# Values of the segments in DRAM: from one row for each token to blocks by group and half, stored whole

## The chip, the cores and the metric

The kernel runs on one core of a Trainium2 chip. The metric is the device time of one execution in microseconds (us). Three runs took 1616.81, 1618.66 and 1619.32 us; the median, 1618.66 us, is the time before. The profile is that of one further execution of 1616.37 us, 1614.70 of them the span from the first to the last instruction.

The engines are named as the profile does: PE (matrix products; PEld is its weight load), DVE (vector), ACT (activations and copies), POOL (general), SP (here nothing but a queue that issues DMAs in order). A name with a q behind it (SPq) is the engine's sequencer.

## What is computed

Four layers one after the other on x of 2048 tokens by 512, in bf16: attention with a recurrent memory (A), a dense layer (B), A again, B again, each on the layer-normed x and added to it. A goes through the tokens in 64 segments of 32:

```
mem = mem0                                   # 8 rows
for s in range(64):
    h = concat(mem, x[32*s : 32*s+32])       # 40 rows of 512
    q, k, v = h @ Wq, h @ Wk, h @ Wv         # 32 heads of 128: 4096 columns each
    p = softmax(mask(q @ k.T * scale))       # for each head 40 x 40
    o = (p @ v) @ Wo                         # back to 512
    mem = o[:8];  outs.append(o[8:])
```

B is `maximum(x @ w1, 0) @ w2` with 1376 columns in between. The memory makes the segments of one layer a chain.

## The kernel before, in words

**Steps.** The program is a chain of 68 steps, k = 0 to 67. In step k the first attention layer works on segment k, and from k = 4 on the second one on segment k - 4 (`layers`, L281), so that two chains share a step. The dense layer of step k is that of segment pair k - 2. A step has the products for queries and keys of half the heads (`qk`, L555: `qp` by L541, its copies QT on ACT L547 and KT on DVE L549), scores `sp` (L575), softmax (L586: `mx`, `es`, `sm`, `P_sb`), the other half likewise, the transposed probabilities (`tp` L617, or a transposing DMA L624), `pv` (L643, weights times the values `Vs`), the product with Wo (`wo` L583 for the memory rows, `wox` L374/L397/L402 for the others), the new memory `mt` and its copies, and last `memory_values(k + 1)` (L715), the values of the memory rows for the next step: two groups `vm` (L724), each copied by ACT into a tile VmS (L728) and stored in DRAM by SP (L729, which issues through `put`, L302).

**Who sets the order.** The instructions of PE, DVE, SP and POOL stand in the order in which the code writes them (`manual_schedule`, L959). Only ACT's order is chosen by the scheduler. Each engine, SP with its DMAs too, takes its instructions strictly one after the other.

**Where the values come from.** `Vs` has for each of the two layers 40 rows of 4096 values. The memory's 8 rows come from `vmd` (L734). The tokens' 32 rows come from DRAM too: for the second layer from `vd1` (`values1`, L342, loaded by L698); for the first layer in steps with k % 4 of 0 or 1 from `vmd` (L703), and in those with k % 4 of 2 or 3 from `vd0[k // 2]` (L706). There the values of a pair of segments (64 tokens) lie, computed ahead by `values0` (L304): one group is 1024 of the 4096 columns, in two halves of 512, one half in partitions 0 to 63 and the other in 64 to 127 of one PSUM tile. ACT copies it to a tile of 128 x 512 (L320), and SP stores each half (64 x 512, 64 KB) into its columns of a DRAM tensor of 64 rows by 4096.

**The first steps.** Step 0 has groups of `values0` for pairs 1, 3 and 5 beside its own work; their copies go to room in the still empty tiles of the dense weights, `w1_sb` and `w2_sb` (`slots`, L809), and their stores are held back (`put` with `later`, L298). In step 1 SP flushes the held stores (L876), 22 of values and 2 of memory values, and then issues the loads of the dense weights (`load_dense`, L156: w1 by L157, w2 by L158 and L160), which overwrite that room and so wait for the stores. Step 1 also has three groups of `values0` of its own (pair 5 group 6, pair 7 groups 0 and 2), whose tiles carry the tag vst, five buffers that VmS, the memory rows `wm` and some inputs use as well. Their 6 stores stand behind the weight loads in SP's queue. Then follow the two VmS stores of `memory_values(2)` at the end of step 1, and in step 2 the load L706, the transposition L289 (`xnT`, the normed tokens that the dense layer's `hp`, L477, reads), the loads L734 and the transposition L624.

**Later steps.** From step 5 on every fourth step (k % 4 = 1) has two to four groups of `values0` (`values_at`, L759).

Of the kernel before, what the change touches and what calls it, by code (L numbers as in the profile page):

```python
# [7 lines left out]
BF = mybir.dt.bfloat16  # L8
# [14 lines left out]
def kernel(  # L23
# [14 lines left out]
    nc = tc.nc  # L38
    _, S, Dm = A_x.shape
    _, H, Dh = A_Wq.shape[0], A_Wq.shape[1], A_Wq.shape[2]  # L40
    M = A_mem0.shape[1]
    SEG = int(A_seg_len)
    Dff = B_w1.shape[1]
    assert Dm == 512 and Dh == 128 and M == 8 and SEG == 32 and H == 32
    L = M + SEG
# [9 lines left out]
    NCH = H * Dh // 512  # L55
# [3 lines left out]
    dram = ctx.enter_context(tc.tile_pool(name="vdram", bufs=2, space=DRAM))  # L59
# [135 lines left out]
    Vs = const.tile([128, H * Dh], BF)  # L195
# [13 lines left out]
    for a in range(2):  # L209
        t = ps_s.tile([128, 512], F32, name=f"sp{a}")  # L210
# [4 lines left out]
    xT0, xnT_tiles, hT_tiles, vd0, vd1, vmds, wm_tiles, wo_tiles, xp_tiles, vp_tiles, obs = {}, {}, {}, {}, {}, {}, {}, {}, {}, {}, {}  # L215
# [82 lines left out]
    def put(later, **store):  # L298
        if later:
            held.append(store)  # L300
        else:
            nc.sync.dma_start(**store)  # L302

    def values0(p, n, lo=0, hi=NC4, pool=None, stage=None):  # L304
        r = 64 * (p % 2)
        if (n, lo) == (0, 0):
            vd0[p] = dram.tile([64, H * Dh], BF, tag="vd0", bufs=3, name="vd0")
        if lo == 0:
            pool, tag = (pool, "wo") if pool else (ps_fill, "fill")
            vp_tiles[p, n] = pool.tile([128, 512], F32, tag=tag, name="vp")  # L310
        vp = vp_tiles[p, n]
        for c4 in range(lo, hi):
            for j in range(2):
                nc.tensor.matmul(vp[64 * j:64 * j + 64, :], lhsT=xT0[p // 2][:, c4, r:r + 64],  # L314
                                 rhs=Wv_sb[:, c4, (n + j) * 512:(n + j + 1) * 512],
                                 start=(c4 == 0), stop=(c4 == NC4 - 1), tile_position=(0, 64 * j))
        if hi < NC4:
            return
        vst = wk.tile([128, 512], BF, tag="vst", bufs=5, name="vst")[:] if stage is None else stage
        nc.scalar.copy(out=vst, in_=vp[:])  # L320
        for j in range(2):
            put(stage is not None, out=vd0[p][:, (n + j) * 512:(n + j + 1) * 512], in_=vst[64 * j:64 * j + 64, :])

    def values_first(ii):

# [369 lines left out]
    def load_values(k, act):  # L695
        for a in act:
            if a == 1 or k == 1:
                nc.sync.dma_start(out=Vs[64 * a + M:64 * a + L, :].rearrange("t (n e) -> t n e", n=NCH),  # L698
                            in_=(vd1.pop(k) if a else vd0[0])[:].rearrange("i j t e -> t (i j) e"))
            elif k >= 4 and k % 4 < 2:  # L700
                for u in range(2):
                    lo = M + 2 * M * u
                    nc.sync.dma_start(out=Vs[lo:lo + 2 * M, :].rearrange("t (n e) -> t n e", n=NCH),  # L703
                                in_=vmds[k - k % 4 - 4 + 2 * (k % 4) + u][:, :, 2 * M:32, :].rearrange("i j t e -> t (i j) e"))
            else:
                nc.sync.dma_start(out=Vs[M:L, :], in_=vd0[k // 2][SEG * (k % 2):SEG * (k % 2) + SEG, :])  # L706

    def tokens_in(k):
        for a in range(2):
# [29 lines left out]
    def block(k, lo, hi):  # L739
        output_x(k - 1, lo, hi)  # L740
        groups = values_at(k)
        if split(k):

            rest = [(i, 0, NC4) for i in range(1, len(groups))]
            if k == 1:
                todo = [] if lo == 0 else [(0, 0, 2)] if hi == 16 else [(0, 2, NC4)] + rest
            else:
                todo = [(0, 0, 2)] if lo == 0 else [(0, 2, NC4)] if hi == 16 else rest
        else:
            todo = [(i, c4, c4 + 2) for i in range(len(groups)) for c4 in range(0, NC4, 2)  # L750
                    if lo < 8 * i + 2 * c4 + 2 <= hi]
        for i, c_lo, c_hi in todo:
            p, n = groups[i]
            values0(p, n, c_lo, c_hi, ps_wo if i in (0, 3 if len(groups) == 4 else 2) else None)
# [51 lines left out]
    def first_step():  # L806
# [5 lines left out]
        with tc.high_priority(offset=PRIO):  # L812
# [4 lines left out]
            memory_values(0, (next(slots), None), (0,))  # L817
            values_second(0, next(slots))
            values0(1, 0, stage=next(slots))
            values0(1, 2, stage=next(slots))  # L820
            m = moments_x(2)
            normalize(nc.vector, xbs[2], xbs[2], m, 0, 128)
# [25 lines left out]
    def step(k):  # L848
# [9 lines left out]
        with tc.high_priority(offset=PRIO):  # L858
            behind = norm_rows.pop(k, None)
            if k == 1:  # L860
                def behind():
                    normalize(nc.vector, xbs[n_x], xbs[n_x], moments_x(n_x), 0, 128)
            qks = qk(0, act, behind=behind)
            load_values(k, act)
            if k == 1:
                memory_values(k)
                inputs_T(n_x, True)
# [91 lines left out]
    with tc.manual_schedule(engines={mybir.EngineType.PE, mybir.EngineType.DVE, mybir.EngineType.SP,  # L959
# [30 lines left out]
        t = xnT_tiles[d + 2] = wk.tile([128, NC4, 128], BF, tag="xnT", bufs=1, name="xnT")  # L990
# [48 lines left out]
```

## Time and profile before

| what | value |
|---|---|
| median of 3 runs | 1618.66 us (1616.81 to 1619.32) |
| profiled execution | 1616.37 us, its span 1614.70 us |
| PE busy | 1568.4 us, 97% of the span |
| DVE, ACT, POOL busy | 1262.5, 738.0, 346.7 us (78%, 46%, 21%) |
| DMA, all queues | 146.41 MB, 91 GB/s in the mean |
| 64 KB stores of values (L302, vd) | 106 from vst tiles and 22 from the weights' room |
| loads L706 (256 KB each) | 32 |

How to read it. The page gives each engine's busy time, its busy share in 40 equal slices of the span (40.4 us each), and the chain of work that ended last, followed back from the last instruction. The waits list who waited for whom: total us, number of times, longest. The timeline has start, duration, engine, line, operation, output<-input and a count of merged instructions; a DMA's row there is the time that SP took to issue it, not the transfer. The chain of waits in order of time has start, duration, and engine or DMA with the line. The table by windows gives the busy time of each engine in a stretch, then three figures: the clock granted to PE (1.00 is full), the busy share of the 16 DMA engines, and GB/s. In the listing of one tile the three figures are minimum, median and maximum in ns of one instruction. The names `vd`, `VmS`, `w_sb` are the tiles with their numbers left out (`w_sb` is w1 or w2).

### The profile page before, as it was taken

Reading aid. Unit: us, or ns where it says so; the run is one execution under the profiler, and the core shown is the slowest. Engines: PE = TensorE matmul, PEld = TensorE weight load, DVE = VectorE, ACT = ScalarE, POOL = GpSimd, SP = SyncE. Lnnn points to the kernel's source line nnn. Section 1 sums busy time; section 2 is a strip of 40 time slices with the busy share of each in tenths; the row PEclk is TensorE's granted clock in tenths of the full one; section 3 lists DMA queues with packets and bytes.
Section 4 is the critical chain, followed back from the end, with each engine's and each line's share of the span. In section 5 each row is a group of like instructions: output and inputs, shape, how many; then the busy total and the mean of one; then the engine's idle time right before and its main releaser. Section 6 shows DMA issues by size and latency. Waiting matters only on the chain.

```text
span 1614.7 us, 94984 instructions
## 1 busy us (share of the span) xinstructions
PE 1568.4 (97%) x42782; PEld 1323.0 (82%) x42782; DVE 1262.5 (78%) x3112; ACT 738.0 (46%) x1800; POOL 346.7 (21%) x666
## 2 busy tenths in 40 slices
PE   6969999999999999999999999999999999999997
PEld 3657888888888888888889888888988888888876
DVE  4548888888888888888888888888888788887865
ACT  3424444454444444444444544445454544545443
POOL 2001122222222222222222222222222222222110
PEclk9979999999999999999999999999999999999999
DMA  9444334443443444343334334443443443334331
GB/s 367 140 132 81 88 63 96 85 83 70 92 86 70 86 90 88 61 94 83 82 75 93 88 65 94 89 83 71 90 92 78 78 87 78 77 76 96 72 67 40
DMA packets 216390, 146.41 MB, mean 91 GB/s; under 512 B 125000, under 2 KB 209328, under 8 KB 214960
## 3 DMA queue, kind: packets, MB, share of 16 engines
q1 hardware_dynamic: 212832, 136.10, 38.4%
q8 instruction: 336, 5.51, 1.5%
q0 software_dynamic: 3072, 4.20, 1.1%
q14 instruction: 70, 0.57, 0.2%
q10 hardware_dynamic: 80, 0.03, 0.0%
HBM read 65.41 MB, written 45.35 MB: 69 GB/s over the span
## 4 chain that ended last, share of the span: by engine, by line
PE 94%; DMA 2%; DVE 1%; SPq 1%; ACT 1%; issue 1%; POOLq 0%; ACTq 0%; DVEq 0%
PE qp L541 37%; PE wox L374 10%; PE wo L583 8%; PE vm L724 7%; PE v L355 7%; PE hp L477 6%; PE sp L500 5%; PE pv L643 4%; PE sp L575 4%; PE vp L314 3%; DMA Wv_sb<-in_A_Wv_dram 2%; PE tp L617 1%; PE xp L448 1%; PE wox L397 1%; DMA vd<-vst 0%
## 5 line engine op out<-in xcount | busy, mean ns | idle before, releaser
L547 ACT CAST QT<-qp 128x480 bf16<-128x480 f32 (+3 forms) x408 | 201.1, 493 | 394.3 <-PE qp L541 394.2
L541 PE MATMUL qp<-HT,Wq_sb 128*128 128x80 bf16 (+1 forms) x8704 | 369.8, 200 | 1.6 <-POOL HT L713 1.2
L541 PE MATMUL qp<-HT,Wk_sb 128*128 128x80 bf16 (+1 forms) x8704 | 369.0, 199 | 2.4 <-DVE KT L549 1.1
L541 PEld LDWEIGHTS <-Wq_sb 128*128 128x128 bf16 x8704 | 326.2, 99 | 33.3 <-issue 25.8
L541 PEld LDWEIGHTS <-Wk_sb 128*128 128x128 bf16 x8704 | 328.7, 100 | 3.6 <-issue 2.7
L549 DVE CAST KT<-qp 128x480 bf16<-128x480 f32 (+3 forms) x408 | 225.1, 565 | 102.1 <-PE qp L541 100.0
L607 POOL TENSOR_TENSOR P_sb<-es,sm 128x320 bf16<-128x320 f32 x185 | 130.5, 719 | 752.5 <-ACT es L597 501.4
L374 PE MATMUL wox<-Wo_sb,OTx 128*64 128x256 bf16 x2880 | 173.6, 273 | 0.0
L591 DVE TENSOR_REDUCE mx<-sp 128x8 f32<-128x320 f32 x256 | 114.7, 487 | 72.4 <-PE sp L575 71.6
L602 DVE TENSOR_REDUCE sm<-es 128x8 f32<-128x320 f32 x256 | 118.9, 465 | 44.3 <-ACT es L597 33.9
L374 PEld LDWEIGHTS <-OTx 128*64 128x64 bf16 x2880 | 150.1, 110 | 2.9
L597 ACT ACTIVATE es<-es 128x320 f32<-128x320 f32 x256 | 110.4, 468 | 60.2 <-DVE es L595 59.5
L724 PE MATMUL vm<-Wv_sb,HTm 128*32 128x512 bf16 x2176 | 136.4, 380 | 0.6 <-DVE HT L793 0.6
L355 PE MATMUL v<-Wv_sb,xnT 128*32 128x512 bf16 x2048 | 129.0, 378 | 0.5 <-PE wo L583 0.5
L583 PE MATMUL wo<-Wo_sb,OTm 128*32 128x512 bf16 x2144 | 128.9, 380 | 0.4 <-issue 0.4
L567 DVE CAST sp<-maskb 128x320 f32<-128x320 bf16 x256 | 118.4, 484 | 0.0
L477 PE MATMUL hp<-xnT,w_sb 128*128 128x64 bf16 (+3 forms) x2948 | 102.7, 193 | 14.4 <-DMA xnT<-XN 14.0
L595 DVE TENSOR_TENSOR es<-sp,mx 128x320 f32<-128x320 f32 x256 | 113.8, 483 | 1.6
L724 PEld LDWEIGHTS <-HTm 128*32 128x32 bf16 x2176 | 90.5, 96 | 27.4 <-issue 12.1
L477 PEld LDWEIGHTS <-w_sb 128*128 128x128 bf16 (+1 forms) x2948 | 95.5, 101 | 15.4 <-issue 9.8
L500 PE MATMUL sp<-w_sb,hT 128*64 128x256 bf16 (+4 forms) x1474 | 106.2, 277 | 0.5 <-ACT hT L483 0.5
L728 ACT CAST VmS<-vm 128x512 bf16<-128x512 f32 x134 | 78.4, 585 | 61.4 <-PE vm L724 54.0
(113 smaller groups left out, 2024.4 us busy)
## 6 DMA issues: line engine op xcount, KB each, us to landing
Vs<-vd SPq DMA_DIRECT2D x96, 256.0 KB
vmd<-VmS SPq DMA_DIRECT2D x134, 128.0 KB
vd<-vst SPq DMA_DIRECT2D x128, 128.0 KB
Vs<-vmd SPq DMA_DIRECT2D x254, 32.0 KB
Vs<-vmd SPq DMA_DIRECT2D x60, 128.0 KB
vd<-vst SPq DMA_DIRECT2D x106, 64.0 KB
Wq_sb<-in_A_Wq_dram SPq DMA_DIRECT2D x2, 2048.0 KB
Wk_sb<-in_A_Wk_dram SPq DMA_DIRECT2D x2, 2048.0 KB
```

The source lines that it names most:

```text
L355: nc.tensor.matmul(vp[32 * j:32 * j + 32, :], lhsT=tokens[:, c4, :], rhs=Wv_sb[:, c4, n * 512:(n + 1) * 512], start=(c4 == 0), stop=(c4 == ...
L374: nc.tensor.matmul(out[64 * j:64 * j + nr, 0:256], lhsT=lhsT, rhs=rhs[:, 256 * j:256 * j + 256], start=start, stop=stop, tile_position=(0, ...
L477: nc.tensor.matmul(hp[0:fs, fc - f0, 0:n], lhsT=w1_sb[:, c4, fc * 128:fc * 128 + fs], rhs=cols(c4), start=(c4 == 0), stop=(c4 == NC4 - 1))
L500: nc.tensor.matmul(sp_banks[bank][64 * j:64 * j + n, 0:w], lhsT=hT_tiles[d][0:fs, fc, 0:n], rhs=w2_flat[0:fs, fc * Dm + 256 * j:fc * Dm + ...
L541: nc.tensor.matmul(qp[:, hi, 0:ncol], lhsT=W_sb[:, c4, h * Dh:(h + 1) * Dh], rhs=HT[:, c4, a_lo:a_hi, :], start=(c4 == 0), stop=(c4 == NC4 ...
L547: nc.scalar.copy(out=dst[:, 0:nh, a_lo * L:a_hi * L], in_=qp[:, 0:nh, 0:ncol])
L549: nc.vector.tensor_copy(out=dst[:, 0:nh, a_lo * L:a_hi * L], in_=qp[:, 0:nh, 0:ncol])
L567: nc.vector.tensor_copy(out=sp_tiles[a], in_=maskb2)
L583: nc.tensor.matmul(wo[32 * j:32 * j + 32, :], lhsT=OTm[:, h, n, 2 * M * c:2 * M * c + 4 * M], rhs=Wo_sb[:, h, :], start=(h < 4), stop=(h > ...
L602: nc.vector.tensor_reduce(out=sm[:], in_=es[:], axis=AX.X, op=ALU.add)
L607: eng.tensor_tensor(out=P, in0=es[:], in1=sm[:].unsqueeze(2).to_broadcast([128, 8, L]), op=ALU.mult)
L724: nc.tensor.matmul(vp[32 * j:32 * j + 32, :], lhsT=HTm[:, c4, :], rhs=Wv_sb[:, c4, n * 512:(n + 1) * 512], start=(c4 == 0), stop=(c4 == NC ...
```

## The change

The DRAM tensor of a pair becomes four blocks (groups) of two halves of 64 tokens by 512 columns, and a group is stored by one DMA of 128 partitions, whose bytes are contiguous in DRAM. The load of a segment's 32 tokens, L706, now reads for each token eight pieces of 512 values (1 KB) where it read one row of 4096 (8 KB). What the loads deliver to `Vs` is the same. 64 stores of 128 KB stand in the place of 128 of 64 KB.

```diff
 def values0(p, n, lo=0, hi=NC4, pool=None, stage=None):
     r = 64 * (p % 2)
     if (n, lo) == (0, 0):
-        vd0[p] = dram.tile([64, H * Dh], BF, tag="vd0", bufs=3, name="vd0")
+        vd0[p] = dram.tile([4, 2, 64, 512], BF, tag="vd0", bufs=3, name="vd0")
...
     nc.scalar.copy(out=vst, in_=vp[:])
-    for j in range(2):
-        put(stage is not None, out=vd0[p][:, (n + j) * 512:(n + j + 1) * 512], in_=vst[64 * j:64 * j + 64, :])
+    put(stage is not None, out=vd0[p][n // 2].rearrange("j t e -> (j t) e"), in_=vst)
...
 def load_values(k, act):
...
         else:
-            nc.sync.dma_start(out=Vs[M:L, :], in_=vd0[k // 2][SEG * (k % 2):SEG * (k % 2) + SEG, :])
+            r = SEG * (k % 2)
+            nc.sync.dma_start(out=Vs[M:L, :].rearrange("t (n e) -> t n e", n=NCH),
+                        in_=vd0[k // 2][:, :, r:r + SEG, :].rearrange("i j t e -> t (i j) e"))
```

In the built program PE, DVE and POOL keep their instructions in the same order. On ACT one instruction stands elsewhere: the second VmS copy of `memory_values(2)` is two QT copies and one `es` earlier, right behind the first `es` of step 2. On SP the stores of values are half as many. SP's DMAs use eight semaphores in turn, so each waits for the one eight places before it; with fewer stores these pairs are others.

## The prediction

> **What bounds the kernel now.** The page first: PE is busy 1568.4 of 1614.7 us (97%), and the chain that ended last is PE for 94%. So a change off PE can win only where PE stands still. The utilisation slices show one dip behind the first 20 us: the third digit of the PE row is 6 (of 9) and that of its clock is 7, so the place is 81 to 121 us. The waits of all engines between 78 and 100 us name it:
>
> ```profile
> PE hp L477 <- DMA xnT<-XN: 14.0, 1, 14.0
> ...
> ACT VmS L728 <- DMA vd<-vst: 7.4, 1, 7.4
> ```
>
> PE waits once, 14.0 us, for the transposed tokens xnT of step 2 (k=2); ACT waits once, 7.4 us, for a store of values that the change touches. Between 130 and 1590 us no wait of PE sums to more than 0.8 us. The chain of waits between 76 and 101 us joins the two:
>
> ```profile
> 82.73 7.34 DMA vd<-vst
> ...
> 90.14 0.59 ACT VmS L728
> ...
> 91.69 3.36 DMA xnT<-XN
> ...
> 95.09 1.55 PE hp L477 x44
> ```
>
> The second VmS copy of memory_values(2) needs a buffer of tag vst, which values0(5,6) filled and whose store has not landed before 90.06. The copy's own store (90.75) stands in SP's queue ahead of the load L706 (91.18) and the transposition L289 (91.69); PE's hp stands behind that. Why the store lands so late is in the timeline of SP from 56 us:
>
> ```profile
> 59.83 9.18 SPq L302 DMA_DIRECT2D vd<-w_sb  x12
> 69.05 0.59 SPq L302 DMA_DIRECT2D vmd<-w_sb  x1
> 69.68 8.18 SPq L302 DMA_DIRECT2D vd<-w_sb  x10
> 77.91 0.59 SPq L157 DMA_DIRECT2D w_sb<-in_B_w_dram  x1
> 79.57 0.39 SPq L158 DMA_DIRECT2D w_sb<-in_B_w_dram  x1
> 80.00 2.18 SPq L160 DMA_DIRECT2D w_sb<-in_B_w_dram  x1
> 82.23 4.14 SPq L302 DMA_DIRECT2D vd<-vst  x6
> ```
>
> SP issues the 22 held stores of 64 KB one after the other without a wait (single ones 0.59 us, one every 0.64 us; 59.83, 67.22, 71.45 and 76.49 are slower ones of 1.1 to 1.8 us). Only then come the dense weights, 2.7 MB, and behind their data the stores of vst. From 69.7 to 78 us the DMA engines are 40% busy (table by windows), so it is SP's issuing that sets the pace. All of 59.83 to 90.1 us is therefore one chain: held stores, weights, store of vst, VmS, xnT, hp.
>
> **The change, part by part.**
>
> *Half the stores.* 128 stores of 64 KB become 64 of 128 KB; 11 of the 22 held ones go, and 3 of the 6 behind the weights. What does a store of 128 rows cost SP? The same operation, 128 x 512 from a vst tile, is there as L360; the listing by tile vd:
>
> ```profile
> L360 SPq DMA_DIRECT2D vd<-vst x128: 338/377/2100, 123.8 to 1585.5; - x128
> L302 SPq DMA_DIRECT2D vd<-vst x106: 445/568/1637, 82.2 to 1476.3; - x106
> L698 SPq DMA_DIRECT2D Vs<-vd x64: 303/328/1802, 128.4 to 1588.1; - x64
> L706 SPq DMA_DIRECT2D Vs<-vd x32: 323/388/1776, 91.2 to 1506.0; - x32
> L302 SPq DMA_DIRECT2D vd<-w_sb x22: 448/596/1784, 59.8 to 76.5; - x22
> ```
>
> (min/median/max ns). The 128-row store issues in less time than the 64-row one. The closest row of them in the timeline is four from 241.79 us, two of L360 and two of VmS: 0.36, 1.85 (one of the slow ones that every line has), 0.38 and 0.40, the last two 0.48 apart. Bounds: 0.43 (0.38 and the 0.05 between two) as the fast end; 0.64, today's pace of the 64-row stores, as the slow end. I take 0.5: DMA engines that are 40% busy with 64 KB every 0.64 us would need about 0.5 us for 128 KB. From 59.83: 12 stores (11 of values, one vmd) x 0.5 = 6.0, plus the 0.9 by which the first at 59.83 is slow today, plus one more slow one (0.5 to 1.2 more than usual; there are three today, in twice as many instructions): 0.7. L157 then issues at 59.83 + 7.6 = 67.4 in place of 77.91, with ends 65.9 (0.43, no other slow one) and 69.6 (0.64 and a slow one of 1.2).
>
> *What follows moves with it.* In before the store of vst lands 90.14 - 77.91 = 12.2 us after L157 was issued (weights at some 350 GB/s, the vst stores behind them). Nothing in the change shortens or lengthens that: w1 waits for the held stores as before, w2 for the last of them. So T, the landing of the store of values0(5,6), is 79.6 (78.1 to 81.8) in place of 90.1.
>
> *ACT's order.* The scheduler moves one instruction: that VmS copy now stands right behind the first es of step 2 (77.09 + 0.47 = 77.56), ahead of two QT copies; all else on PE, DVE, ACT and POOL keeps its place. Behind it wait QT (78.06 today) and with it PE's next qp (77.98). So PE stops at 78.0 instead of 81.1, but only until VmS is done, T + 0.6 = 80.2; the rest of qp, wox and sp, 2.7 us (78.47 to 81.13 today), then ends at 82.9. From the landing to hp it is 95.09 - 90.14 = 4.95 us as today (VmS 0.59, its store, L706, xnT 3.36): hp at 84.5. xnT is still last, by 1.6 us. The transposition also waits for w2, since SP's DMAs use eight semaphores in turn; w2 lands ahead of T. hp goes from 95.09 to 84.5: **10.5 us less** (8.3 to 12.0).
>
> *PE's clock.* The table by windows:
>
> ```profile
> 95.10:100.30 5.20, 5.20 (x100) 4.06 (x101) 0.00 (x0) 0.69 (x3) 0.00 (x0) 0.54 0.25 58
> ...
> 115.30:118.80 3.50, 3.50 (x102) 3.01 (x100) 2.17 (x5) 1.05 (x4) 0.28 (x2) 1.00 0.63 136
> ```
>
> After the stall the granted clock (third figure from the end) is 0.54, and what PE does between hp and the next tp takes 5.2 us; the same 100 instructions of step 3 take 3.5 us at 1.00. This 1.7 us is won if the shorter stops (2.2 and 1.6 us, some 4 in all) leave the clock alone, and not if they lower it. The row can't decide it, so I take half, 0.9, and both ends for the range. The Trainium skill (TensorE: Matmul & The Clock Gate, Part 1) has the clock halved after an idle window of about 3.4 us; by that rule two stops of about 2 us would leave it, and the sum would be 0.8 us better. The trace agrees in so far as 14 us of idling did lower it.
>
> *The load.* L706 (32 of them) reads 8 pieces of 1 KB for each of 32 rows in place of one row of 8 KB. L698 has that form already; it issues no slower (rows above) and stands right ahead of the transposition in most steps; PE never waits for xnT there. Between issue of L289 and hp lie 4.9 us in step 3 and 5 to 8 later, and it needs 3.4. Taken at nothing; the cover is 1.5 us in step 3, more elsewhere, and Vs itself is read at the end of the step. Against it speaks that the pieces are eight times as many: the Trainium skill (DMA: Bandwidth & Descriptors, on why a DMA's semaphore counts 16) has one descriptor for each contiguous run. By a cost for each run the loads would be later, but L698's rows show no waiter.
>
> *Later stores.* In steps 5, 9, 13 ... 3 or 4 stores go, from a queue that waits for ACT and POOL anyway: nothing for PE.
>
> **Sum.** 10.5 + 0.9 = 11.4 us. The profiled execution took 1616.37 us (span 1614.70 and 1.67 around it): it would be 1605.0. The median of the runs is 1618.66, 2.3 above that execution; against it 1607.3.
>
> **Rivals.**
>
> *The store costs by its rows* (the change doesn't do what it says). If 128 rows cost SP twice 0.6 us in a long run, the queue is no shorter: 12 x 1.24 + 0.9 = 15.8, L157 at 75.6, gain 2.3, 1616.4; or none, 1618.7. For it: long runs of such stores aren't in the trace, four is the most. Against: its third and fourth take 0.38 and 0.40, no more than one alone (0.34 to 0.38). 7%.
>
> *Another wait holds xnT.* Say PE's stop at 78 is longer, or w2 lands later under a faster stream of stores, and a third of the gain goes: 1611 to 1614. For it: xnT leads by 1.6 us alone. 7%.
>
> *The loads in pieces delay the transposition* (the slower side). If each of the 32 loads puts xnT past the start of hp, PE loses in 32 steps: with a usual margin of 7 - 3.4 = 3.6 us, the point where the gain is eaten is 11.4/32 = 0.36 us past it, that is xnT 4.0 us later than now; 4.2 us later gives 32 x 0.6 = 19 and 1626. For it: it stands directly ahead in the queue. Against: L698, same bytes and pieces, same place, no wait. 4%.
>
> **How the numbers follow.** Forecast 82%: 1607.3, by the ends of its terms 1618.66 - 12.0 - 1.7 = 1605.0 to 1618.66 - 8.3 = 1610.4. The runs shown lie 1.9 below and 0.7 above their median, so the range is 1603.5 to 1612.0. Anything under 0.2% (3.2 us) can't be told from no change here. Faster: 82 and most of the second rival, 88%; same 8%; slower 4%.
>
> **What would show it.** Right: 11 held stores between 60 and 67 us at about 0.5 us each; L157 near 67; VmS near 80; hp of step 2 near 84.5; PE's wait for xnT 1 to 3 us in place of 14.0, with one of 2 to 3 us for ACT at qp ahead of it; all steps after that of the old length. Wrong: stores of 1 us and more, hp of step 2 later than 88, or a wait for xnT in later steps.

## The result and the profile after

Five runs of the changed kernel took 1608.92 to 1612.6 us, median 1609.73 us; five of the kernel before 1616.81 to 1619.81, median 1618.66. The ratio of the new time to the old is 0.9949, with a 95% interval of 0.9935 to 0.9964: 8.9 us faster where 11.4 were forecast, 2.4 us above the predicted 1607.3 and inside the range. The profiled execution took 1608.92 us, its span 1607.2.

The slices of the page show where. The third digit of the PE row, 6 before, is now 8, and that of its clock 8 in place of 7; the second digit, 9 before, is 8, since what is left of the stop begins earlier:

```profile
PE   6889999999999999999999999999999999999997
...
PEclk9989999999999999999999999999999999999999
```

(Lines behind L322 have numbers one lower after the change, and lines behind the load, which is two lines longer now, one higher: L289 and L706 keep theirs, hp is L476, qp L540, VmS L729.) SP's timeline from 59 us, start, time to issue, line, DMA, count:

```profile
59.72 0.34 SPq L302 DMA_DIRECT2D vmd<-w_sb  x1
60.11 3.96 SPq L302 DMA_DIRECT2D vd<-w_sb  x6
64.12 0.45 SPq L302 DMA_DIRECT2D vmd<-w_sb  x1
64.61 4.25 SPq L302 DMA_DIRECT2D vd<-w_sb  x5
68.96 0.39 SPq L157 DMA_DIRECT2D w_sb<-in_B_w_dram  x1
```

Eleven stores take 8.2 us where 22 took 17.4, and the weights are issued at 68.96 us instead of 77.91. The listing of tile vd (minimum, median and maximum in ns) has them at 0.45 us in the median; with the pause behind it, one comes every 0.49 us:

```profile
L302 SPq DMA_DIRECT2D vd<-w_sb x11: 424/447/2288, 60.1 to 68.4; - x11
```

Two are slow, 1.54 us at 60.58 and 2.29 at 66.09; four were slow before.

The chain of waits between 66 and 96 us has the same links as before, 8 to 10 us earlier:

```profile
68.42 1.88 DMA vd<-w_sb
...
73.24 7.47 DMA vd<-vst
...
80.73 0.59 ACT VmS L729
...
82.25 4.84 DMA xnT<-XN
...
87.13 1.55 PE hp L476 x44
```

The store of vst lands at 80.71 (before 90.06) and hp starts at 87.13 (before 95.09): 7.96 us. One link got longer: from the issue of the transposition to its landing it was 3.36 us and is 4.84. The waits between 70 and 90 us show what became of PE's single one of 14.0:

```profile
PE hp L476 <- DMA xnT<-XN: 2.4, 1, 2.4
...
PE qp L540 <- ACT VmS L729: 2.3, 1, 2.3
ACT VmS L729 <- DMA vd<-vst: 2.0, 1, 2.0
...
PE sp L574 <- issue: 0.8, 1, 0.8
```

Two stops of 2.3 and 2.4 us, the first for the copy that moved forward on ACT, the second for xnT. Between 130 and 1580 us no wait of PE sums to more than 0.8 us, as before. PE's clock in the table by windows (the third figure from the end of each row):

```profile
76.00:79.10 3.10, 2.30 (x86) 2.15 (x83) 1.35 (x3) 0.77 (x2) 0.00 (x0) 1.00 1.05 343
79.10:81.37 2.27, 0.00 (x0) 0.00 (x0) 0.60 (x3) 0.64 (x2) 1.26 (x2) 0.83 0.47 161
81.37:84.75 3.38, 3.38 (x88) 2.76 (x88) 1.13 (x3) 0.50 (x2) 0.46 (x2) 0.50 1.13 178
84.75:87.10 2.35, 0.00 (x2) 0.04 (x1) 1.67 (x4) 0.47 (x1) 0.00 (x0) 0.50 0.44 55
87.10:91.70 4.60, 4.57 (x96) 3.66 (x95) 0.49 (x1) 0.69 (x3) 0.00 (x0) 0.59 0.34 48
```

The clock falls within the first stop of 2.27 us and stays at 0.50 beyond the second. The stretch from hp to the next tp takes 4.6 us, where it took 5.2 and would take 3.5 at full clock. The clock was low from 80.60 to 90.84 us, 10.24 us in all; before, it was low for 17.07.

### The profile page after: what moved, and what is told of

Its sections match the earlier page's. It is cut to its first block, busy times and chain, and to the rows that moved or that the text cites. A ratio compares the mean times of both kernels' runs of the same rounds, so it can differ in the third digit from the quotient of the medians.

```text
span 1607.2 us, 94867 instructions
## 1 busy us (share of the span) xinstructions
PE 1570.6 (98%) x42782; PEld 1324.2 (82%) x42782; DVE 1262.9 (79%) x3112; ACT 738.7 (46%) x1800; POOL 347.6 (22%) x666
## 4 chain that ended last, share of the span: by engine, by line
PE 94%; DMA 3%; SPq 1%; DVE 1%; issue 1%; ACT 0%; POOLq 0%; ACTq 0%; DVEq 0%
PE qp L540 37%; PE wox L373 10%; PE wo L582 8%; PE vm L725 7%; PE v L354 7%; PE hp L476 6%; PE sp L499 5%; PE pv L642 4%; PE sp L574 4%; PE vp L314 3%; DMA Wv_sb<-in_A_Wv_dram 2%; PE tp L616 1%; PE xp L447 1%; SPq L302 1%; DMA vd<-vst 0%
## 5 line engine op out<-in xcount | busy, mean ns | idle before, releaser
L540 PE MATMUL qp<-HT,Wk_sb 128*128 128x80 bf16 (+1 forms) x8704 | 369.8, 200 | 3.8 <-ACT VmS L729 2.3
L540 PE MATMUL qp<-HT,Wq_sb 128*128 128x80 bf16 (+1 forms) x8704 | 370.1, 200 | 2.4 <-POOL HT L714 1.2
L540 PEld LDWEIGHTS <-Wq_sb 128*128 128x128 bf16 x8704 | 326.2, 99 | 34.2 <-issue 26.7
L540 PEld LDWEIGHTS <-Wk_sb 128*128 128x128 bf16 x8704 | 328.9, 100 | 5.2 <-issue 4.0
L476 PE MATMUL hp<-xnT,w_sb 128*128 128x64 bf16 (+3 forms) x2948 | 102.8, 193 | 3.4 <-DMA xnT<-XN 2.4
L729 ACT CAST VmS<-vm 128x512 bf16<-128x512 f32 x134 | 78.6, 586 | 56.0 <-PE vm L725 53.9
L476 PEld LDWEIGHTS <-w_sb 128*128 128x128 bf16 (+1 forms) x2948 | 95.6, 101 | 4.5 <-issue 3.8
```

The lines of the kernel that those rows point to most:

```text
L476: nc.tensor.matmul(hp[0:fs, fc - f0, 0:n], lhsT=w1_sb[:, c4, fc * 128:fc * 128 + fs], rhs=cols(c4), start=(c4 == 0), stop=(c4 == NC4 - 1))
L540: nc.tensor.matmul(qp[:, hi, 0:ncol], lhsT=W_sb[:, c4, h * Dh:(h + 1) * Dh], rhs=HT[:, c4, a_lo:a_hi, :], start=(c4 == 0), stop=(c4 == NC4 ...
```

## The experiments

**Theory:** the whole gain is SP's time for the held stores of step 1, which sets when the weights, the store behind them, VmS, xnT and hp of step 2 come. **Rivals:** the layout itself, the later steps, the wait of ACT taken alone, the pieces of the load. Each experiment is compared with runs of the kernel before taken beside it (medians 1617.74 to 1618.53 us).

**e1: blocks, but two stores for each group.**

```diff
-        put(stage is not None, out=vd0[p][n // 2].rearrange("j t e -> (j t) e"), in_=vst)
+        for j in range(2):
+            put(stage is not None, out=vd0[p][n // 2, j], in_=vst[64 * j:64 * j + 64, :])
```

> The layout of the changed kernel (blocks by group and half, loads in 1 KB pieces), but each half stored by a DMA of its own, 64 KB, contiguous in DRAM: 128 stores as before. Theory 'number of stores': SP issues the 22 held stores one every 0.64 us as before the change, L157 near 77.9 us, hp of step 2 near 95, and the time is that of before, 1618.7 us within 1.5. Rival 'layout': it is the contiguous bytes that make a store cheap to issue; 22 stores at about 0.45 us leave L157 near 71 us and give 1611 to 1614.

1619.47 us, ratio 1.0008 (0.9999 to 1.0016): as before. The listing of tile vd (min/median/max ns) has the same cost for the now contiguous 64 KB as for strided rows:

```profile
L360 SPq DMA_DIRECT2D vd<-vst x128: 338/377/1919, 122.1 to 1586.2; - x128
L302 SPq DMA_DIRECT2D vd<-vst x106: 445/587/1659, 81.2 to 1477.1; - x106
...
L302 SPq DMA_DIRECT2D vd<-w_sb x22: 454/596/1306, 60.0 to 75.8; - x22
```

L157 is at 76.46 us, hp waits 13.1 us for xnT. The contiguous layout saves nothing; the number of stores does, and one of 128 rows (0.45 us in a row) is cheaper than one of 64 (0.60). This kernel has all 32 loads in pieces as well, and is not measurably slower for it.

**e2 and e3: the change for early pairs alone, and for late pairs alone.**

```diff
+    def whole(p):
+        return p < 8        # e3: p > 8
...
+        if whole(p):
+            put(stage is not None, out=vd0[p][n // 2].rearrange("j t e -> (j t) e"), in_=vst)
+        else:
+            for j in range(2):
+                put(stage is not None, out=vd0[p][:, (n + j) * 512:(n + j + 1) * 512], in_=vst[64 * j:64 * j + 64, :])
```

The tile and the load of a pair go by the same condition.

> The change for pairs 1, 3, 5 and 7 alone (all that is stored in steps 0 and 1, and three groups of step 5); pairs from 9 on keep rows of 8 KB and two stores. Theory 'the queue of step 1 alone': as the changed kernel, 1609.7 us within 1.5. Rival 'the later steps win or lose too' (stores saved there, loads in pieces): off the changed kernel by more than 1.5 us, to 1613 where half the gain came later, to 1607 where the loads in pieces cost something later.

> The opposite: pairs 1 to 7 as before the change, pairs from 9 on changed. Theory 'the queue of step 1 alone': 1618.7 us within 1.5, hp of step 2 near 95 us. Rival 'later steps': 1614 to 1616 where they win, above 1621 where the loads in pieces cost.

e2: 1610.54 us, 0.9955 (0.9942 to 0.9968); e3: 1619.37 us, 1.0007 (0.9998 to 1.0016). The early pairs give what the whole change gives, the late ones nothing. Stores saved and loads cut up in later steps are worth nothing that can be measured.

**e4: the held stores issued twice.** The second copy goes to DRAM that nobody reads, so the kernel moves 1.4 MB more than it needs.

```diff
+        if stage is not None:
+            again = dram.tile([2, 64, 512], BF, tag="again", bufs=12, name="again")
+            put(True, out=again[:].rearrange("j t e -> (j t) e"), in_=vst)
```

> The changed kernel with each of the 11 held stores of values issued twice, the second time to a DRAM tensor that nobody reads: SP's queue of step 1 has 11 more stores of 128 KB. Theory: each adds its 0.49 us and the slow ones grow with the instructions, so L157 comes 5.4 to 7.5 us later and the end 5.4 to 7.5 us later than the changed kernel, 1615 to 1617. Rival 'SP's queue is not what decides' (the weights or the clock do): within 1.5 us of the changed kernel.

1614.62 us, 0.9974 (0.9962 to 0.9985): 4.9 us above the changed kernel, a little below the 1615 to 1617 expected and outside the rival's 1.5; by the profiled executions it is 2.9. L157 is issued at 73.94 us, 5.0 later (5.4 to 7.5 expected), and the transposition at 87.54, 5.3 later. hp comes only 3.6 later, at 90.76, since xnT needs 3.22 us here where it needed 4.88 in the changed kernel.

**e5 to e8: the order of the weights.** In e5 and e7 `load_dense()` moves behind the stores of the vst tiles in step 1, on the changed kernel and on the kernel before; in e6 and e8 w2 also goes behind the transposition of step 2.

```diff
-        if k == 1:
-            load_dense()
...
             block(k, mid, H)
+            if k == 1:
+                load_dense()
...
             transpose_step(k)
+            if k == 2:
+                load_dense2()        # e6, e8: the two loads of w2
```

> The changed kernel with the loads of the dense weights issued later in step 1, behind the stores of the three vst tiles. The scheduler then puts the second VmS copy of step 2 ahead of that step's queries, and its store of vst lands near 71 us. Theory 'one chain': ACT's wait at VmS goes, but the data of xnT still stand behind those of w2 (issued near 72, landed near 82), so hp of step 2 comes at 83 to 85 us in place of 87.1: 1605.5 to 1608. Rival 'ACT's wait is all there is': hp at 81 to 82 without a wait, 1602 to 1604.

> As the one before, and w2 (both loads) issued only in step 2 behind the transposition. Theory 'one chain': nothing but w1 is ahead of xnT in the DMA queues, hp starts when its turn comes, near 81.3 us, PE's clock stays at 1.00, and 5.7 + 1.2 us are won: 1602 to 1604; w2 then lands near 85 us, just when its products start, which may cost up to 2 us of it. Rival 'the transfers only move': PE waits for w2 as long as it waited for xnT, 1608 to 1610.

> The kernel before the change (rows of 8 KB, two stores) with the weights issued behind the vst stores. The store that VmS waits for then lands near 80 us in place of 90. Theory 'one chain from SP's issues': it does not help, since w1 and w2 come 4 us later (L157 near 82) and xnT's data behind theirs, hp near 95: 1617 to 1620. Rival 'the wait of ACT for the store of vst is the cause' (the one that the waits name): hp near 85, 1609 to 1611.

> The kernel before the change with the weights behind the vst stores and w2 behind the transposition of step 2. Theory: the 22 stores still put w1 at 82 us, landed near 88, and hp then: 1611 to 1613, which is 8 to 10 us above the same order with whole stores (the difference that the halved queue makes, here of 22 and 6 stores against 11 and 3). Rival: with w2 out of the way the stores no longer matter, and both orders give the same time within 2 us.

e5: 1610.7 us, 0.9951 (0.9939 to 0.9963). e6: 1607.91 us, 0.9943 (0.9929 to 0.9957). e7: 1618.3 us, 1.0005 (0.9994 to 1.0015). e8: 1617.03 us, 0.9991 (0.9981 to 1.0).

e7 is as the theory had it. VmS starts at 80.22 us there, ten earlier than before, and nothing is won: hp starts at 95.45. The wait of ACT for the store was thus a link of the chain and not its cause: with VmS ten us earlier xnT is issued at 88.0, and its data still stand behind weights that came later (L157 at 81.25; the DMA engines move 342 and 381 GB/s in the two stretches of 2 us from 88 to 92). e8 missed by 4 us (hp at 91.66, expected near 88) but keeps the order of whole and half stores: 9.1 us between e8 and e6.

e5 and e6 fell short of the theory. In e5 ACT's wait for the store is gone and hp starts at 84.34 us, inside the 83 to 85 forecast; the matrix products of the new memory in step 2 (`mt`) start 2.7 us earlier than in the changed kernel (92.88 for 95.62). In the time this is not seen: by step 30 the profiled execution had lost it again against that of the changed kernel, and why is open. Ahead of hp PE stops once, for 3.2 us, with no cause that the waits name.

In e6 xnT is issued at 74.04 us, and PE waits for neither xnT nor the weights; its waits between 74 and 96 us:

```profile
PEld L542 <- issue: 3.5, 1, 3.5
PE qp L542 <- issue: 3.4, 1, 3.4
...
PE sp L576 <- issue: 1.3, 1, 1.3
```

(qp is L542 there.) It stops for 1.3 us at 75.85 and for 3.4 us at 81.35 for nothing that a semaphore tells, the second time while w2 is on its way (the DMA engines move 283 GB/s from 78 to 81.3 us and 216 from 81.3 to 84.8). `mt` starts at 95.47 us, so that nothing is won over the changed kernel. The DMA queues have, from 81.3 to 84.8 us, one packet of 16 KB for instructions in it:

```profile
q8 instruction: 1, 0.02, 1.9%
```

A late load of PE's own code, held up by DMA engines full of weights, would fit; before the change such a packet, at 83.06 us, fell into the 14 us in which PE stood still anyway. It is inferred: no run here moved the code loads alone.

**e9: the load behind the transposition (step 2).**

```diff
+            if k != 2:
+                load_values(k, act)
...
             transpose_step(k)
+            if k == 2:
+                load_values(k, act)
```

> The changed kernel with the load of values of step 2 (L706, 256 pieces of 1 KB) issued behind the transposition instead of ahead of it. In the changed kernel xnT took 4.84 us from issue to hp where it took 3.36 before. Theory 'the pieces are not it': xnT is issued 0.45 us earlier and takes as long as the runs so far show with pieces ahead of it (3.2 to 5.9), 1608 to 1610. Rival 'the pieces delay the transposition': it takes 3.4 or less and 2 us are won, 1607 to 1608, hp at 85 us.

1607.73 us, 0.9943 (0.9929 to 0.9957). Against the changed kernel that is 2 us less, with intervals that overlap. xnT is issued at 80.95 and hp starts at 85.22. The time and hp are where the rival had them, the 4.27 us between issue and hp are in the range of the theory, so this run alone decides nothing. Of the 1.9 us by which hp is earlier 0.8 come from SP's queue, which was that much ahead at VmS (79.92 for 80.73), and 0.5 from the place of the load.

From issue to hp (0.04 us longer than to the landing) e1 and e4, with pieces ahead of xnT, need 3.45 and 3.22 us; so the pieces are not enough to make it long. What the long ones share is a packet of 16 KB of the instruction queue q8 between the issue and hp, one each in the changed kernel (4.88), e2 (5.96), e9 (4.27) and e11 (4.64). The short ones, before (3.40), e1, e3 (3.22) and e4, have none of q8; before, e1 and e3 have one of 8 KB of the other instruction queue, q14. In e7 (7.43) there is none of q8 either, but the data of w2 stand ahead of xnT. With nine packets of q8 between 50 and 100 us in the changed kernel some of this can be chance. Whether it is that packet or what comes with it stays open.

**e10 and e11: the held stores from two queues.** Every second one is issued by POOL, on the changed kernel and on the kernel before.

```diff
-            while held:
-                put(False, **held.pop(0))
+            for i in range(len(held)):
+                (nc.gpsimd if i % 2 else nc.sync).dma_start(**held.pop(0))
```

> The changed kernel with every second held store issued by POOL instead of SP: the same DMAs from two queues. Theory 'SP's queue time': SP has 7 stores in place of 13, L157 near 66 us in place of 69, hp of step 2 2 to 3 us earlier than in the changed kernel. If nothing else stops PE this gives 1606 to 1608. Rival, from the two runs that reordered the weights: PE then meets its code loads behind the weights' data, and as much goes to waits without a named cause (issue): 1608.5 to 1611.

> The kernel before the change (128 stores of 64 KB in rows) with every second held store issued by POOL. Theory 'SP's queue time': SP has 12 held stores at 0.64 us in place of 24, and without any change of layout L157 comes at 69 to 73 us and the end at 1610 to 1614; the upper end if POOL needs about 1 us for each of its 12. Rival 'the number or the form of the stores in the DMA engines': no gain, 1617 to 1620.

e11: 1608.36 us, 0.9945 (0.9932 to 0.9957). The kernel before, its rows and its 128 stores untouched, wins as much as the change does, and more than the 1610 to 1614 expected. SP's timeline:

```profile
60.46 0.34 SPq L877 DMA_DIRECT2D vmd<-w_sb  x1
60.85 8.66 SPq L877 DMA_DIRECT2D vd<-w_sb  x11
69.88 0.41 SPq L157 DMA_DIRECT2D w_sb<-in_B_w_dram  x1
```

The weights come at 69.88 us, 0.9 behind the changed kernel. POOL has nothing else in its timeline there and issued its twelve from 54.97 to 61.4 us, most of them before SP began.

e10: 1605.32 us, 0.9936 (0.9920 to 0.9953), the lowest median of all, though two of the six runs took 1611; its interval overlaps that of the change. L157 is at 64.67, hp at 82.62 (4.5 us earlier where 2 to 3 were expected), and between 74 and 96 us PE waits for no DMA:

```profile
PE sp L574 <- issue: 1.3, 1, 1.3
PE mt L780 <- ACT wm L774: 0.5, 1, 0.5
PE vm L725 <- DVE HT L794: 0.4, 1, 0.4
```

Set side by side, in us (`mt` is the start of the products of the new memory in step 2, which stand behind the stop):

| run | L157 issued | `mt` of step 2 | profiled execution | median |
|---|---|---|---|---|
| before | 77.91 | 104.13 | 1616.37 | 1618.66 |
| e1 | 76.46 | 102.47 | 1617.12 | 1619.47 |
| e4 | 73.94 | 99.12 | 1611.79 | 1614.62 |
| e11 | 69.88 | 96.38 | 1609.49 | 1608.36 |
| the change | 68.96 | 95.62 | 1608.92 | 1609.73 |
| e10 | 64.67 | 89.84 | 1604.95 | 1605.32 |

13.2 us of queue are 14.3 us at `mt` and 13.3 us of the median. Single pairs fit less well: what is left from `mt` to the end of the span takes 1510.3 (e7) to 1514.7 us (e5) in the profiled executions, and why is open. Two us at the end can thus not be read from one profile.

## Why the prediction was right, and where it was too high

*The bound and the chain: right.* The single stop in step 2, its links, and that it hung on SP's issuing. e2, e3, e4 and e11 show it each in its own way.

*The store's price: right.* 0.5 us taken, 0.49 measured. The rival that it costs by its rows is refuted by that row.

*The slow issues: too small.* Here the step failed that put 1.6 us (0.9 and 0.7) on the slow ones: they took 1.1 and 1.8 more than usual, 2.9, and the first store was 0.3 later. L157 came at 68.96 in place of 67.4. The row of before had the sizes (up to 1.78 in that stretch), and the forecast took one more of 0.7, low in its own range of 0.5 to 1.2, because there are half as many instructions. But the slow issues did not halve with the stores: beyond the usual 0.6 they took 3.4 us in the 22 stores of before, and beyond the usual 0.45 they took 2.9 in the 11 of after.

*From L157 to VmS, behind the landing of the store:* 12.2 taken, 11.8 measured (68.96 to 80.73). This term went the other way.

*From VmS to hp: too small.* "4.95 us as today" became 6.40, all of it the transposition (4.84 for 3.36). No rival had this: the second lets another wait hold xnT, the third lets the pieces ahead delay it, and with those pieces ahead e1 and e4 are short. The cause stays open (e9 and the runs beside it). The order on PE and ACT was right: stops of 2.2 and 1.6 us forecast, 2.3 and 2.4 measured, xnT last.

*The clock: nearer to the lower end.* Half of 1.7 taken; 0.6 us is what hp to tp is shorter, and nothing shows that the shorter stops spared the clock. It fell after 1.5 us of a stop, and it rose 3.7 us behind the start of hp where it rose 4.8 behind it before. That half of it came near is luck in part: in the traces of all 13 kernels a stretch at 0.50 that ends inside the span lasts 3.41 us or a multiple of it (17.07 before, 10.24 here, 3.41 in e10), so where hp falls in that beat counts too. The rule of the Trainium skill (TensorE: Matmul & The Clock Gate, Part 1), an idle window of some 3.4 us, would have kept it at 1.00 here; the trace speaks against that reading. In e10 it falls after 1.35 us without a matmul:

```profile
73.00:76.00 3.00, 2.90 (x102) 2.52 (x99) 1.58 (x4) 0.65 (x2) 0.00 (x0) 1.00 0.92 311
76.00:77.40 1.40, 0.05 (x5) 0.00 (x0) 0.00 (x0) 0.58 (x1) 0.00 (x0) 0.99 0.08 21
77.40:80.80 3.40, 3.40 (x104) 3.35 (x104) 1.95 (x5) 1.08 (x3) 0.38 (x1) 0.50 0.67 158
```

*The load at nothing: right* (e1, e2 against the change). The slower rival would have needed xnT 4 us later in every such step; the changed kernel waits for xnT once, in step 2. Nor is there any measurable cost of eight descriptors in place of one, which the Trainium skill's rule (DMA: Bandwidth & Descriptors, on why a DMA's semaphore counts 16) had as a possibility. *Later stores at nothing: right* (e3).

Sum: 1.6 - 0.5 + 1.5 = 2.6 us is what hp came later than forecast (87.13 for 84.5). By the profiled executions the gain is 7.5 us, by the medians 8.9; the five runs alone lie 3.7 us apart, and pv of step 2, with 8.5 us (100.66 to 92.15), lies between them.

The range has a slip in its sum: 1605.0 and 1610.4, with 1.9 below and 0.7 above, are 1603.1 to 1611.1, not 1603.5 to 1612.0. The measured median lies in both.

## What to carry to other kernels

In a kernel bound by one engine, look for the one place where that engine stands still and follow the chain back past the wait that is named: here the wait was for a store, its cause a queue of 22 small DMAs issued 12 to 30 us earlier, ahead of a large load. Count such a queue in DMAs and the time between their issues, not in bytes: 128 KB took 0.49 us here and 64 KB 0.64. Fewer DMAs, or a second idle queue, brought the same. And a stall that goes can uncover what it had hidden, here waits of PE of 1.3 to 3.4 us without a named cause (e5, e6, e10). The shortfall of the forecast itself lay in single links of the chain, the slow issues and the transposition, which were taken at the size of one other execution.

## What the runs showed of the hardware that was not expected

A store of 64 partitions by 1 KB takes SP longer to issue than one of 128: 0.60 against 0.45 us in a close row, whether its DRAM side is strided (before) or contiguous (e1). Why is open. Among them come issues of 1 to 2.3 us, four in the 24 held stores of before and two in the 13 of the change. At each of these six a packet of 16 KB of the instruction queue q8 was under way, and no such packet fell into the two rows without a slow issue; the same holds for the rows of e2, e3 and e4. The changed kernel between 66 and 68.4 us, with the slow one of 66.09:

```profile
q1 hardware_dynamic: 287, 0.25, 32.3%
q8 instruction: 1, 0.02, 4.7%
```

That SP waits for its code there is likely and not shown. Nor was it expected that PE's clock falls after a stop of only 1.35 us (e10). The length of the stop alone does not tell when: in e3 the clock fell 4.0 us into a stop of 14.4, and in e9, after two stops of 1.2 us and one of 2.2, it fell 1.3 us after PE had gone on. In all 13 traces it changes only at steps of 3.41 us from one another.
